# Five-stage chunk pipeline in phase A, second half of s4 issued one block later, LayerNorm statistics and evictions partly on ScalarE

## The chip, the cores and the metric

The kernel runs on one core of one Trainium2 chip. The metric is device time in microseconds (us) of a whole execution; lower is better. All times are medians of several executions. PE is the matmul engine, DVE the vector engine, ACT the scalar engine, POOL the general-purpose engine, SP the engine that issues most transfers.

Three terms recur. *Phase A* is the convolution. *The hand-over* is the stretch from the last phase-A matmul to the first matmul of s2. *Block distance* is the time from the first s2 matmul of one block to that of the next. s1(0) stands for the first s1 matmul of the first block, s1(1) for that of the second, s2(0) for the first s2 matmul.

## The reference

```python
x = A_q                                              # 2048 x 1024, bf16
for layer in range(2):
    x = x + layernorm(x) * conv(A_k, A_v)            # "A": the same conv result y both times
    z = layernorm(x); xb = z                         # "B": a mixer and an MLP
    h  = gelu(layernorm(z) @ w1)                     # 1024 -> 1024        (s1)
    xb = xb + shift4(h) @ w2                         # rows shifted by -1,+1,-2,+2  (s2)
    xb = xb + gelu(layernorm(xb) @ w3) @ w4          # 1024 -> 3584 (s3) -> 1024 (s4)
    x = x + xb
```

The convolution is a long one along the sequence, done in the kernel as FFT-like products of small matrices. Note that LayerNorm is applied to `z`, which is itself the output of a LayerNorm.

## The kernel before

Phase A works on eight chunks of 128 columns and writes y to a scratch tensor in DRAM. Two Python generators per chunk give slots of work. Most working tiles have one buffer, and the transposes share one PSUM buffer:

```python
wk  = es.enter_context(tc.tile_pool(name="a_wk", bufs=1))     # zs, z2, tm, ut ...
ptp = es.enter_context(tc.tile_pool(name="pa_t", bufs=1, space=PSUM))
# ... h_stream(c), x_stream(c): generators, one yield per stage, started 4 slots apart
```

After phase A, eight steps (2 layers x 4 blocks of 512 rows) go through these parts (shortened):

```python
def ln_stats4(src_fn):           # DVE bn_stats, bn_aggr; POOL add, pow; DVE nmr
def normalize(dst, src, rstd, nmr, t):   # ACT: Identity with scale and bias

def transposes(dst_tile, xn_tile):
    for t in range(TPB):                                   # 4 tiles of 128 rows
        pt = ps_t.tile([P, KC, P], BF16, tag="pt")         # PSUM, two buffers
        for k in range(KC):
            nc.tensor.transpose(pt[:, k, :], xn_tile[:, t, k * P:(k + 1) * P], ident[:])
        nc.vector.tensor_copy(dst_tile[:, :, t * P:(t + 1) * P], pt[:])

def pre_dve(layer, b):           # loads x and y, then
    # stats(x) -> xn0 -> x += xn0*y -> stats(x) -> xB = norm(x) -> stats(xB) -> xn
def pre_pe(layer, b):  # transposes of xn, the operand of s1
def s2_mm(layer, b):   # 64 matmuls; DVE adds; stats(xB) -> xn1 (ACT); x += xB (DVE)
def s2_pe(layer, b):   # transposes of xn1, the operand of s3
def s4(layer, b):      # two halves of 512 columns, 112 matmuls each; four DVE adds after each

for i in range(n):
    s2_mm(*steps[i])
    if i + 2 < n:
        pre_pe(*steps[i + 2]); s1(*steps[i + 2])
    s2_pe(*steps[i])
    s3(*steps[i])
    if i + 3 < n:
        pre_dve(*steps[i + 3])
    s4(*steps[i])
```

The order of the source is a priority, not the final order: the compiler's scheduler orders the instructions on each engine. The traces show the final order.

Of the kernel before, what the change touches and what calls it, by code (L numbers as in the profile page):

```python
# [87 lines left out]
def _phase_a(tc, k_in, v_in, shift_k, ssm_k, ssm_D, y_dram, ident):  # L88
# [6 lines left out]
    with ExitStack() as es:  # L95
        cp = es.enter_context(tc.tile_pool(name="a_const", bufs=1))
        inp = es.enter_context(tc.tile_pool(name="a_in", bufs=2))
        wk = es.enter_context(tc.tile_pool(name="a_wk", bufs=1))
        wk2 = es.enter_context(tc.tile_pool(name="a_wk2", bufs=2))
        bfp = es.enter_context(tc.tile_pool(name="a_bf", bufs=3))  # L100
# [31 lines left out]
        def stage1(x_c, zs):  # L132
            for a4 in range(NA // 4):
                ps = pmm2.tile([P, 4, 2, DC], F32, tag="mm2")
                for ai in range(4):
                    a = a4 * 4 + ai
                    for r in range(2):
                        nc.tensor.matmul(ps[:, ai, r, :], fwd[:, a, r, :], x_c[:, a, :], start=True, stop=True)  # L138
                asl = slice(a4 * 4, (a4 + 1) * 4)
                if RELAYOUT == "xbar":  # L140
                    evac(zs[:, :, asl, :].rearrange("p q a m -> p a q m"),
                         ps[:].rearrange("p a r (g q) -> p a q (r g)", g=G4))
                else:
                    evac(zs[:, :, asl, :].rearrange("p m a q -> p a m q"),
                         ps[:].rearrange("p a r (g q) -> p a (r g) q", g=G4))

        def relayout(zs, z2, eng):
            if RELAYOUT == "xbar":
                nc.sync.dma_start_transpose(out=z2[:], in_=zs[:].rearrange("p q a m -> p (q a m)"))
                return  # L150
            zr = zs[:].rearrange("p m a q -> p (m a q)")
            for q8 in range(NQ // 8):
                pt = ptp.tile([P, 8, P], BF16, tag="pt")
                for qi in range(8):
                    nc.tensor.transpose(pt[:, qi, :], zr[:, _sl(q8 * 8 + qi, P, NQ)], ident[:])
                evac(z2[:, q8 * 8:(q8 + 1) * 8, :], pt[:], eng)

        def zs_tile(tag):
            if RELAYOUT == "xbar":
                zt = wk.tile([P, NQ, NA, 2 * G4], BF16, tag=tag, name=tag)  # L160
            else:
                zt = wk.tile([P, 2 * G4, NA, NQ], BF16, tag=tag, name=tag)
            return zt

        def h_stream(c):
            cols = slice(c * DC, (c + 1) * DC)
            hk_c = inp.tile([P, S], BF16, tag="hk_c")
            nc.gpsimd.dma_start(hk_c[:], hv_[:, c, :])
            h_c = wk.tile([P, NA, DC], BF16, tag="h_c")
            for a8 in range(NA // 8):  # L170
                pt = ptp.tile([P, 8, P], BF16, tag="pt")
                for ai in range(8):
                    nc.tensor.transpose(pt[:, ai, :], hk_c[:, _sl(a8 * 8 + ai, P, NA)], ident[:])
                nc.vector.tensor_copy(h_c[:, a8 * 8:(a8 + 1) * 8, :], pt[:])
            nc.vector.tensor_tensor(h_c[0:1, 0, :], h_c[0:1, 0, :], dt_[0:1, cols], op=ALU.add)
            yield
            zs = zs_tile("zs_h")
            stage1(h_c, zs)
            yield
            z2 = wk.tile([P, NQ, P], BF16, tag="z2_h")  # L180
            relayout(zs, z2, "act")
            yield
            yield
            bf = bfp.tile([P, NQ, P], BF16, tag="bf")
            for blk in range(NBLK):
                bs = slice(blk * 4, (blk + 1) * 4)
                ps = pmm_d.tile([P, 4, P], F32, tag="mm")
                nc.tensor.matmul(ps[:], W_B, z2[:, bs, :], start=True, stop=True)
                evac(bf[:, bs, :], ps[:], "dve")
            bf_tiles[c] = bf  # L190
            yield

        bf_tiles = {}

        def x_stream(c):
            cols = slice(c * DC, (c + 1) * DC)
            k_nat = inp.tile([P, NT, DC], BF16, tag="k_nat")
            nc.gpsimd.dma_start(k_nat[:], kv_[:, :, cols])
            v_c = inp.tile([P, NA, DC], BF16, tag="v_c")
            nc.gpsimd.dma_start(v_c[:], vv_[:, :, cols])  # L200
# [7 lines left out]
            yield  # L208
            x_c = wk.tile([P, NA, DC], BF16, tag="x_c")
# [8 lines left out]
            yield  # L218
            zs = zs_tile("zs_x")
            stage1(x_c, zs)  # L220
            yield
            z2 = wk.tile([P, NQ, P], BF16, tag="z2_x")
            relayout(zs, z2, "dve")
            yield
            yield
            bf = bf_tiles.pop(c)
            tm1 = wk.tile([P, NQ, P], BF16, tag="tm1")
            tm2 = wk.tile([P, NQ, P], BF16, tag="tm2")
# [8 lines left out]
            yield  # L237
# [9 lines left out]
            yield  # L247
            y_c = wk2.tile([P, NA, DC], BF16, tag="y_c")
            for a8 in range(NA // 8):
# [5 lines left out]
                evac(y_c[:, a8 * 8:(a8 + 1) * 8, :], ps[:].rearrange("p a g q -> p a (g q)"), "act")  # L255
            nc.gpsimd.dma_start(yv_[:, :, cols], y_c[:])
            yield

        hs = {c: h_stream(c) for c in range(NCH)}
        xs = {c: x_stream(c) for c in range(NCH)}  # L260
        starts = []
        for c in range(NCH):
            starts.append((4 * c - 6, 1, c, hs[c]))
            starts.append((4 * c, 0, c, xs[c]))
        t_first = min(st[0] for st in starts)
        active = []
        slot = t_first
        pending = sorted(starts, key=lambda st: (st[0], st[1], st[2]))
        while pending or active:
            while pending and pending[0][0] <= slot:  # L270
                active.append(pending.pop(0))
            for item in list(active):
                try:
                    next(item[3])
                except StopIteration:
                    active.remove(item)
            slot += 1


def _b_layers(ctx, tc, x_src, y_dram, w1, w2, w3, w4, out, consts, n_layers=2):  # L280
# [16 lines left out]
    x_all = big.tile([P, NT, D], BF16, name="x_all")  # L297
# [9 lines left out]
    xv = x_src.rearrange("(t p) d -> p t d", p=P)  # L307
# [3 lines left out]
    def ln_stats4(src_fn):  # L311
        st = small.tile([P, TPB, 2, 6], F32, tag="st")
        mv = small.tile([P, TPB, 2], F32, tag="mv")
        for t in range(TPB):
# [5 lines left out]
        nc.gpsimd.tensor_scalar(ve[:], mv[:, :, 1], EPS, None, op0=ALU.add)  # L320
        rstd = small.tile([P, TPB], F32, tag="rstd")
        nc.gpsimd.tensor_tensor(rstd[:], ve[:], mhalf[:], op=ALU.pow)  # L322
        nmr = small.tile([P, TPB], F32, tag="nmr")
        nc.vector.scalar_tensor_tensor(nmr[:], mv[:, :, 0], -1.0, rstd[:], op0=ALU.mult, op1=ALU.mult)  # L324
        return rstd, nmr

    def normalize(dst, src, rstd, nmr, t):
        nc.scalar.activation(dst, src, ACT.Identity, bias=nmr[:, t:t + 1], scale=rstd[:, t:t + 1])  # L328

    def transposes(dst_tile, xn_tile):  # L330
        for t in range(TPB):
            pt = ps_t.tile([P, KC, P], BF16, tag="pt")
            for k in range(KC):
                nc.tensor.transpose(pt[:, k, :], xn_tile[:, t, k * P:(k + 1) * P], ident[:])  # L334
            nc.vector.tensor_copy(dst_tile[:, :, t * P:(t + 1) * P], pt[:])  # L335
# [3 lines left out]
    def pre_dve(layer, b):  # L339
        first = layer == 0  # L340
        T0 = b * TPB
        yt = xio.tile([P, TPB, D], BF16, tag="yt")
        for t in range(TPB):
            if first:
                nc.sync.dma_start(x_all[:, T0 + t, :], xv[:, T0 + t, :])
            nc.sync.dma_start(yt[:, t, :], yv[:, T0 + t, :])
        rstd, nmr = ln_stats4(lambda t: x_all[:, T0 + t, :])
        xn0 = xio.tile([P, TPB, D], BF16, tag="xn0")
        for t in range(TPB):
            normalize(xn0[:, t, :], x_all[:, T0 + t, :], rstd, nmr, t)  # L350
            nc.vector.tensor_tensor(xn0[:, t, :], xn0[:, t, :], yt[:, t, :], op=ALU.mult)  # L351
            nc.vector.tensor_tensor(x_all[:, T0 + t, :], x_all[:, T0 + t, :], xn0[:, t, :], op=ALU.add)  # L352
        rstd, nmr = ln_stats4(lambda t: x_all[:, T0 + t, :])
        for t in range(TPB):
            normalize(xB_all[:, T0 + t, :], x_all[:, T0 + t, :], rstd, nmr, t)
        rstd, nmr = ln_stats4(lambda t: xB_all[:, T0 + t, :])
        xn = xnp.tile([P, TPB, D], BF16, tag="xn")
        for t in range(TPB):
            normalize(xn[:, t, :], xB_all[:, T0 + t, :], rstd, nmr, t)
        state[("xn", layer, b)] = xn  # L360

    def pre_pe(layer, b):
        xnT = xtp.tile([P, KC, TB], BF16, tag="xT")
        transposes(xnT, state.pop(("xn", layer, b)))
# [54 lines left out]
    def s4(layer, b):  # L419
        h2T = state.pop(("h2T", layer, b))  # L420
        last = layer == n_layers - 1
        for half in range(2):
# [13 lines left out]
        if last:  # L436
            for t in range(TPB):
                T = b * TPB + t
                nc.sync.dma_start(ov[:, T, :], x_all[:, T, :])
# [10 lines left out]
    for i in range(n):  # L450
        s2_mm(*steps[i])
        if i + 2 < n:
# [6 lines left out]
        s4(*steps[i])  # L459
# [3 lines left out]
def kernel(  # L463
# [35 lines left out]
    _b_layers(ctx, tc, q2, y_dram[:], B_w1, B_w2, B_w3, B_w4, out2, consts)  # L499
# [30 lines left out]
```

## Time and profile before

The time before was 1462.93 us (median of 5).

| stretch | from | to | us |
|---|---|---|---|
| phase A | 0 | 283.5 | 283.5 |
| hand-over | 283.5 | 370.8 | 87.3 |
| eight blocks | 370.8 | 1461.9 | 1091.1 |

From the page of the kernel before: busy time of the engines, and the span in 40 slices, with tenths of busy time for PE and tenths of full clock for PEclk.

```profile
PE 1284.9 (88%) x7763; PEld 677.2 (46%) x7872; DVE 540.8 (37%) x1043; ACT 457.6 (31%) x562; POOL 72.9 (5%) x100
PE   3698998626899989998999899989989998998998
PEclk9799999958999999999999999999999998999999
```

The hand-over lies in the eighth to tenth slice. In the ninth PE is busy for between two and three tenths of the time, at a mean clock of 0.5. After it every third or fourth slice dips.

POOL timeline before (start, duration, what was issued; in brackets the wait before it). Chunks leave phase A 29 us apart (the last two gaps are shorter), the first at 98.6 us:

```profile
98.61 1.17 POOL L256 DMA_DIRECT2D y_scratch<-y_c  x1
127.69 1.13 POOL L256 DMA_DIRECT2D y_scratch<-y_c  x1
285.01 1.12 POOL L256 DMA_DIRECT2D y_scratch<-y_c  x1 [16.05 <-ACT y_c L128]
```

PE timeline before, in a middle block, where s2 (L397) ends and the transposes of xn (L334) begin:

```profile
796.03 10.52 PE L397 MATMUL ps<-wt,hT 128*128 128x512 bf16 x48 [0.26 <-DMA wt<-in_B_w_dram]
806.61 0.78 PE L334 MATMUL pt<-ident,xn 128*128 128x128 bf16 x11
810.15 0.61 PE L334 MATMUL pt<-ident,xn 128*128 128x128 bf16 x8 [2.76 <-DVE xnT L335]
811.83 1.71 PE L334 MATMUL pt<-ident,xn 128*128 128x128 bf16 x16 [1.07 <-DVE xnT L335]
```

The transposes wait for DVE to empty PSUM, and DVE is still busy with the adds and statistics of s2 before it comes to a copy (DVE timeline before, the same moments, two lines of many):

```profile
808.14 0.69 DVE L317 BATCH_NORM_STATS2 st<-xB_all 128x6 f32<-128x512 bf16 x1
809.46 0.64 DVE L335 COPY xnT<-pt 128x1024 bf16<-128x1024 bf16 x1
```

The three largest waits of PE before, from 365 us to the end, that is, over the eight blocks (us in total, how often, the longest):

```profile
PE pt L334 <- DVE xnT L335: 20.8, 12, 2.8
PE pt L334 <- ACT xn L328: 12.0, 3, 5.1
PE ps L375 <- DVE xn1T L335: 8.0, 8, 1.2
```

DVE and SP timelines before, at the hand-over: first statistics, normalisers ready, yt issued, first product with y.

```profile
286.24 0.69 DVE L316 BATCH_NORM_STATS2 st<-x_all 128x6 f32<-128x512 bf16 x1 [2.48 <-DMA x_all<-in_A_q_dram]
293.23 1.75 SPq L346 DMA_DIRECT2D yt<-y_scratch  x4
294.42 0.16 DVE L324 SCALAR_TENSOR_TENSOR nmr<-mv,rstd 128x4 f32<-128x4 f32 x1 [1.48 <-POOL rstd L322]
295.95 0.69 DVE L351 TENSOR_TENSOR xn<-xn,yt 128x1024 bf16<-128x1024 bf16 x1 [1.37 <-ACT xn L328]
```

Measured from the last phase-A matmul at 283.5, statistics begin after 2.7 us and the product with y after 12.4 us.

### The profile page before, as it was taken

How to read it: one execution, taken by the hardware profiler on the slowest of the kernel's cores; microseconds unless marked ns; L12 is line 12 of the kernel's file. 1: busy time of each engine (PE TensorE's matmuls, PEld its weight loads, DVE VectorE, ACT ScalarE, POOL GpSimd, SP SyncE). 2: the span in 40 equal slices, each digit the busy share in tenths (PEclk: the TensorE clock that was granted, in tenths of full speed). 3: DMA queues.
4: the chain of work that ended last, by engine and by line, in shares of the span. 5: the costliest groups of instructions: out<-in, count | busy, mean ns of one | idle time of the engine just before them, and what ended most of it. 6: DMA issues, size and time to landing. Idle time of an engine off the chain costs nothing.

```text
span 1461.9 us, 18065 instructions
## 1 busy us (share of the span) xinstructions
PE 1284.9 (88%) x7763; PEld 677.2 (46%) x7872; DVE 540.8 (37%) x1043; ACT 457.6 (31%) x562; POOL 72.9 (5%) x100
## 2 busy tenths in 40 slices
PE   3698998626899989998999899989989998998998
PEld 2577776413444444444444444444444443443443
DVE  2487878578740082028103800460040005004001
ACT  2455564346552035104510540063013201300310
POOL 1011110011100000001000100010000000000000
PEclk9799999958999999999999999999999998999999
DMA  9222320233345534544353445434443543455333
GB/s 278 59 59 60 86 60 16 75 128 114 117 149 168 156 109 140 172 144 143 117 173 116 144 144 162 137 105 144 159 158 115 158 154 120 144 163 163 108 114 115
DMA packets 166434, 188.03 MB, mean 129 GB/s; under 512 B 6225, under 2 KB 153809, under 8 KB 166098
## 3 DMA queue, kind: packets, MB, share of 16 engines
q1 hardware_dynamic: 161602, 169.05, 36.5%
q0 software_dynamic: 4608, 16.78, 4.1%
q8 instruction: 61, 1.00, 0.3%
q10 hardware_dynamic: 144, 1.05, 0.2%
q14 instruction: 19, 0.16, 0.0%
HBM read 178.46 MB, written 8.39 MB: 128 GB/s over the span
## 4 chain that ended last, share of the span: by engine, by line
issue 66%; PE 7%; POOL 3%; DVE 2%; ACT 2%; DMA 0%; POOLq 0%; SPq 0%; DVEq 0%; ACTq 0%
PE ps L375 4%; PE s L430 3%; POOL rstd L322 2%; ACT xn L328 1%; DVE st L316 1%; DVE st L317 1%; POOL ve L320 1%; DMA x_all<-in_A_q_dram 0%; ACT xB_all L328 0%; PE pt L334 0%; DVE xn L351 0%; DVE x_all L352 0%; DVE x_all L434 0%; DVE xnT L335 0%; DVE mv L318 0%
## 5 line engine op out<-in xcount | busy, mean ns | idle before, releaser
L375 PE MATMUL ps<-xn1T,wt 128*128 128x512 bf16 x1752 | 396.7, 386 | 14.8 <-DVE xn1T L335 8.0
L430 PE MATMUL s<-wt,h2T 128*128 128x512 bf16 x1760 | 387.9, 379 | 2.1
L375 PEld LDWEIGHTS <-wt 128*128 128x128 bf16 x2304 | 230.1, 100 | 305.1 <-issue 50.4
L434 DVE TENSOR_TENSOR x_all<-x_all,s 128x512 bf16<-128x512 bf16 x64 | 39.7, 682 | 722.6 <-PE s L430 722.6
L430 PEld LDWEIGHTS <-h2T 128*128 128x128 bf16 x1792 | 175.0, 98 | 211.9 <-issue 1.2
L328 ACT ACTIVATE xn<-xB_all,nmr,rstd 128x1024 bf16<-128x1024 bf16 x64 | 75.2, 1229 | 494.6 <-DVE nmr L324 490.5
L377 ACT ACTIVATE h2T<-ps 128x512 bf16<-128x512 f32 x224 | 133.4, 595 | 231.4 <-PE ps L375 217.6
L375 PE MATMUL ps<-xnT,wt 128*128 128x512 bf16 x499 | 122.5, 404 | 6.8 <-ACT hT L377 3.9
L334 PE MATMUL pt<-ident,xn 128*128 128x128 bf16 x512 | 48.6, 252 | 84.4 <-ACT xn L328 57.1
L397 PE MATMUL ps<-wt,hT 128*128 128x512 bf16 x497 | 113.0, 379 | 4.8 <-DMA wt<-in_B_w_dram 3.4
L334 PEld LDWEIGHTS <-xn 128*128 128x128 bf16 x512 | 38.8, 113 | 97.8 <-ACT xn L328 64.1
L397 PEld LDWEIGHTS <-hT 128*128 128x128 bf16 x512 | 49.9, 98 | 65.2 <-issue 7.6
L320 POOL TENSOR_SCALAR ve<-mv 128x4 f32<-128x4 f32 x32 | 7.3, 228 | 1023.6 <-DVE mv L318 1011.5
L377 ACT ACTIVATE hT<-ps 128x512 bf16<-128x512 f32 x64 | 37.8, 591 | 33.6 <-PE ps L375 33.5
L316 DVE BATCH_NORM_STATS2 st<-xB_all 128x6 f32<-128x512 bf16 x64 | 43.8, 684 | 11.6 <-ACT xB_all L328 11.1
L328 ACT ACTIVATE xB_all<-x_all,nmr,rstd 128x1024 bf16<-128x1024 bf16 x32 | 38.1, 1230 | 27.2 <-DVE nmr L324 27.2
L138 PEld LDWEIGHTS <-fwd 128*128 128x128 bf16 x512 | 35.7, 101 | 23.5 <-issue 17.8
L128 ACT ACTIVATE ut<-ps 128x1024 bf16<-128x1024 f32 x32 | 32.7, 1021 | 44.2 <-PE ps L244 44.2
L128 ACT ACTIVATE zs_x<-ps 128x1024 bf16<-128x1024 f32 x32 | 30.9, 1023 | 49.0 <-PE ps L138 49.0
L399 DVE TENSOR_TENSOR xB_all<-xB_all,ps 128x512 bf16<-128x512 bf16 x64 | 43.2, 675 | 7.1 <-PE ps L397 7.1
L328 ACT ACTIVATE xn<-x_all,nmr,rstd 128x1024 bf16<-128x1024 bf16 x32 | 38.9, 1233 | 21.1 <-DVE nmr L324 21.1
L316 DVE BATCH_NORM_STATS2 st<-x_all 128x6 f32<-128x512 bf16 x64 | 43.0, 672 | 4.0 <-DMA x_all<-in_A_q_dram 3.8
(62 smaller groups left out, 1084.5 us busy)
## 6 DMA issues: line engine op xcount, KB each, us to landing
wt<-in_B_w_dram SPq DMA_DIRECT2D x72, 1024.0 KB, 5.3
wt<-in_B_w_dram SPq DMA_DIRECT2D x144, 512.0 KB, 3.6
yt<-y_scratch SPq DMA_DIRECT2D x32, 256.0 KB, 3.8
hk_c<-in_A_ssm_k_dram POOLq DMA_DIRECT2D x8, 512.0 KB, 4.2
k_nat<-in_A_k_dram POOLq DMA_DIRECT2D x8, 512.0 KB, 5.9
v_c<-in_A_v_dram POOLq DMA_DIRECT2D x8, 512.0 KB, 5.5
y_scratch<-y_c POOLq DMA_DIRECT2D x8, 512.0 KB, 4.4
x_all<-in_A_q_dram SPq DMA_DIRECT2D x16, 256.0 KB, 5.7
```

Source lines behind the costliest of these rows:

```text
L128: nc.scalar.activation(dst, src, ACT.Copy)
L138: nc.tensor.matmul(ps[:, ai, r, :], fwd[:, a, r, :], x_c[:, a, :], start=True, stop=True)
L316: nc.vector.bn_stats(st[:, t, 0, :], src[:, 0:512])
L322: nc.gpsimd.tensor_tensor(rstd[:], ve[:], mhalf[:], op=ALU.pow)
L328: nc.scalar.activation(dst, src, ACT.Identity, bias=nmr[:, t:t + 1], scale=rstd[:, t:t + 1])
L334: nc.tensor.transpose(pt[:, k, :], xn_tile[:, t, k * P:(k + 1) * P], ident[:])
L375: nc.tensor.matmul(ps[:], wt[:, k, mi * P:(mi + 1) * P], xT[:, k, :], start=(k == 0), stop=(k == KC - 1))
L377: nc.scalar.activation(dst_fn(m), ps[:], ACT.Gelu_apprx_tanh)
L397: nc.tensor.matmul(ps[:], hT[:, k, c0:c0 + P], wts[half * 2 + k // 4][:, k % 4, :], start=(k == 0), stop=(k == KC - 1))
L399: nc.vector.tensor_tensor(xB_all[:, T, half * 512:(half + 1) * 512], xB_all[:, T, half * 512:(half + 1) * 512], ps[:], op=ALU.add)
L430: nc.tensor.matmul(pss[t][:], h2T[:, f, t * P:(t + 1) * P], wt[:, fi, :], start=(f == 0), stop=(f == FC - 1))
L434: nc.vector.tensor_tensor(x_all[:, T, half * 512:(half + 1) * 512], x_all[:, T, half * 512:(half + 1) * 512], pss[t][:], op=ALU.add)
```

## The change

It has three intents: keep more chunks of phase A in flight; shorten the hand-over; and cover the gap after s2 with matmuls of the previous block. Cut to its core:

```diff
 # phase A
-bfp = tile_pool("a_bf", bufs=3)
+wkx = tile_pool("a_wkx", bufs=2)      # zs, z2, x_c, tm1, tm2 now have two buffers
+bfp = tile_pool("a_bf", bufs=2)
-# h_stream / x_stream, one yield per stage
+# g1..g5, one yield per PSUM tile; round r runs g5(r-4), g4(r-3), g3(r-2), g2(r-1), g1(r) in turn
 # loading x
-    nc.sync.dma_start(x_all[:, T0 + t, :], xv[:, T0 + t, :])       # 16 x 256 KB, in pre_dve
+    for i in range(4):                                             # 4 x 1 MB, after phase A
+        nc.scalar.dma_start(x_all[:, i*4:(i+1)*4, :], qv[:, i*4:(i+1)*4, :])
 # transposes: eviction
-    nc.vector.tensor_copy(...)
+    if t % 2 == 0: nc.vector.tensor_copy(...)
+    else:          nc.scalar.activation(..., ACT.Copy)
 # pre_dve
+    # block 0 only: tile by tile, its stages staggered ("fine"), transposes included
-    normalize(xB_all[...], x_all[...], rstd, nmr, t)
-    rstd, nmr = ln_stats4(xB_all)                                  # third statistics, DVE
+    normalize(xB_all[...], x_all[...], rstd, nmr, t, accum=sum3[:, t:t+1])
+    nc.scalar.activation(xn[:, t, :], xB_all[...], ACT.Square, accum_out=sq3[:, t:t+1])
+    rstd, nmr = act_stats_finish(sum3, sq3)                        # six POOL operations
 # main loop
     s2_mm(*steps[i])
+    if i > 0: s4(*steps[i - 1], halves=(1,))
     ... pre_pe, s1, s2_pe, s3, pre_dve as before ...
-    s4(*steps[i])
+    s4(*steps[i], halves=(0,))
+s4(*steps[n - 1], halves=(1,))        # after the loop
```

## The prediction

> **What bounds the kernel now.** By the timeline, three stretches.
>
> *Phase A, 0 to 284 us.* y_scratch writes leave every 29.0 us per chunk; the first at 98.6. From the cadences, a chunk needs about 24 us of PE (320 matmuls of 128 columns at 0.056 to 0.064 us, 24 of 512 at 0.214), 22 of DVE (36 evictions at 0.60), 17 of ACT (18 at 0.93). No engine is full: 5 us per chunk is slot structure with single buffers. Start and drain cost more: PE does little before 23 us, and the clock is 0.61 at 40-60 us.
>
> *Hand-over, 284 to 371 us* (last phase-A matmul to first L397 matmul). PE work there is about 33 us; the table by stretches shows 2 us of PE in each of 280-300 and 300-320. The chain is stats, POOL rstd (1.04), ACT normalise (1.23 each), three times for four tiles; yt is issued only 9.6 us after the last matmul, behind the last y write.
>
> *Eight MLP blocks.* First L397 matmuls are 140.0 us apart; the matmuls need about 130 (0.219 us per 512 columns). The Trainium skill (TensorE: Matmul & The Clock Gate, Part 1) gives 0.2157 warm and a half clock after idling; the trace agrees (0.219; clock 0.74 in 1220-1240). The 10 us gap lies just after s2: transposes wait for DVE, busy with s2's adds and stats (xnT up to 2.8 us), and in the last two blocks for ACT xn (5.1 each), then run at half clock (32 transposes in 4.4 us instead of 2.2).
>
> **What the change does.**
> 1. Phase A: five groups of different chunks issued round-robin, most buffers doubled, same instructions. Steady chunk 29 to about 25.5 us, PE-bound; filling and draining stay latency-bound (pt has one buffer, about 1.8 us per use, 12 uses per chunk). The larger pools probably stop w1/w2 loading at the start, relieving the first inputs (skt took 15 us). Last matmul at about 252 instead of 283: -32.
> 2. Hand-over: block 0 per tile; third stats move from DVE (25 to 19 us per block) to ACT (12 to 16 passes of 1.23) and POOL. Yet yt still waits for the last y write, and x_all becomes 4 MB at once. Block 0 gains perhaps 3 us; blocks 1 and 2, begun meanwhile, about 10. ACT becomes the limit. -13.
> 3. s4's second half (112 matmuls, 24 us) moves after the next s2, covering s2's DVE/ACT chain of about 12 us and keeping the clock up. New: its first w4 tile waits for a wdn buffer of w2 (about 1 us), and half the transposes get ACT's slower eviction (1.02 against 0.69). Net -5 per block in the middle, -7 in the last two: -42 in all.
>
> Sum: 1463 - 32 - 13 - 42 = **1376 us**, range 1340 to 1412. Chances: faster 0.93, within 2% 0.06, slower 0.01.
>
> **What would show it.** y writes 25 to 26 us apart, last phase-A matmul near 250; first L397-type matmul 73 to 78 us after that; s2 starts 134 to 136 us apart with clock near 1.00; waits of PE for DVE xnT nearly gone; ACT busy up by about 40 us, DVE down by about 45; mean clock 0.97.
>
> **What would make it wrong.** The compiler's scheduler already reorders instructions, so phase A may keep its 29 us if pt or PSUM buffers are the true limit; or it may drain far better. The 4 MB x_all load may delay the y write and yt by several us. ACT, with gelu plus 16 long passes, could hold PSUM and stall s3. If the accumulating activations cost more than 1.23 us, or an activation table is reloaded per switch, there is no gain at the hand-over.

## The result

The changed kernel takes 1436.62 us (median of 9), against 1462.8 us of the kernel before on the same chip: ratio 0.9822, 95% interval 0.9806 to 0.9838. The prediction was 1376 us, and the measured time lies outside its range.

| stretch | before | predicted | after |
|---|---|---|---|
| phase A | 283.5 | about -32 | 254.7 (-28.8) |
| hand-over | 87.3 | about -13 | 96.8 (+9.5) |
| eight blocks | 1091.1 | about -42 | 1084.0 (-7.1) |

From the page after:

```profile
PE 1266.1 (88%) x7761; PEld 668.6 (47%) x7872; DVE 476.5 (33%) x913; ACT 522.6 (36%) x690; POOL 87.7 (6%) x162
PE   2799998057799989998999899989999999999998
PEclk9999999577899999999999999999999999999999
```

The dip of the hand-over is still there, and in one slice PE is busy for less than a tenth of the time. POOL timeline after: chunks leave 25.8 us apart while the pipeline is full, the first one 17.8 us later than before and the last one 29 us earlier.

```profile
116.40 1.12 POOL L275 DMA_DIRECT2D y_scratch<-y_c  x1 [1.43 <-ACT y_c L129]
142.20 1.12 POOL L275 DMA_DIRECT2D y_scratch<-y_c  x1 [1.09 <-ACT y_c L129]
256.14 1.12 POOL L275 DMA_DIRECT2D y_scratch<-y_c  x1 [9.62 <-ACT y_c L129]
```

PE timeline after, in a middle block (L495 is s4, L366 the transposes, L440 s1 and s3):

```profile
767.96 24.33 PE L495 MATMUL s<-wt,h2T 128*128 128x512 bf16 x109 [0.59 <-DMA wt<-in_B_w_dram]
794.82 0.27 PE L366 MATMUL pt<-ident,xn 128*128 128x128 bf16 x2 [0.64 <-DVE xnT L368]
813.10 0.61 PE L366 MATMUL pt<-ident,xn 128*128 128x128 bf16 x8 [1.72 <-DVE xn1T L368]
816.72 0.58 PE L440 MATMUL ps<-xn1T,wt 128*128 128x512 bf16 x1 [1.22 <-ACT xn1T L370]
```

s4 does fill the place after s2. But there are waits again, now at the transposes of xn1 and at the start of s3. The three largest waits of PE after, and that for xnT, same stretch and columns as before:

```profile
PE pt L366 <- DVE xn1T L368: 11.2, 10, 1.7
PE ps L440 <- ACT xn1T L370: 11.1, 8, 2.5
PE s L495 <- DMA wt<-in_B_w_dram: 9.2, 7, 2.1
PE pt L366 <- DVE xnT L368: 4.1, 6, 0.9
```

The waits named in the prediction (xnT 20.8, xn 12.0 us) have shrunk. But others stand in their place: these four lines sum to 36 us, the three of before to 41, and all waits of PE in this stretch, most of them not shown here, come to 59 us before and after. Block distances in the middle are 140.2, 142.5, 140.6 and 143.5 us, where 140.0 was before and 134 to 136 was predicted.

At the hand-over (DVE and SP timelines after; L454 is the load of w2):

```profile
251.00 2.04 SPq L454 DMA_DIRECT2D wt<-in_B_w_dram  x4
264.49 0.69 DVE L331 BATCH_NORM_STATS2 st<-x_all 128x6 f32<-128x512 bf16 x1 [9.61 <-DMA x_all<-in_A_q_dram]
265.55 1.77 SPq L378 DMA_DIRECT2D yt<-y_scratch  x4
271.37 0.69 DVE L399 TENSOR_TENSOR xn<-xn,yt 128x1024 bf16<-128x1024 bf16 x1 [2.53 <-DMA yt<-y_scratch]
```

From the last phase-A matmul at 254.7, statistics begin after 9.8 us (2.7 before) and the product with y after 16.7 us (12.4 before).

### The profile page after: what moved, and what is told of

Read it like the earlier page. It is cut to its first block, busy times and chain, and to the rows that moved or that the text cites. A ratio compares the mean times of both kernels' runs of the same rounds, so it can differ in the third digit from the quotient of the medians.

```text
span 1435.4 us, 18057 instructions
## 1 busy us (share of the span) xinstructions
PE 1266.1 (88%) x7761; PEld 668.6 (47%) x7872; DVE 476.5 (33%) x913; ACT 522.6 (36%) x690; POOL 87.7 (6%) x162
## 4 chain that ended last, share of the span: by engine, by line
PE 56%; ACT 8%; DVE 8%; DMA 5%; POOL 2%; issue 1%; another core or an unknown queue 1%; DVEq 0%; SPq 0%; ACTq 0%
PE ps L440 27%; PE s L495 25%; PE ps L462 4%; DMA wt<-in_B_w_dram 4%; ACT xn L344 2%; DVE st L332 2%; ACT xB_all L344 2%; DVE st L331 1%; ACT xn L406 1%; POOL rstd L337 1%; ACT xn1T L370 1%; DVE x_all L499 1%; DVE xn L399 1%; DVE x_all L400 1%
## 5 line engine op out<-in xcount | busy, mean ns | idle before, releaser
L440 PE MATMUL ps<-xn1T,wt 128*128 128x512 bf16 x1752 | 396.1, 385 | 19.4 <-ACT xn1T L370 11.1
L495 PE MATMUL s<-wt,h2T 128*128 128x512 bf16 x1755 | 389.1, 381 | 11.3 <-DMA wt<-in_B_w_dram 9.2
L440 PEld LDWEIGHTS <-wt 128*128 128x128 bf16 x2304 | 229.1, 99 | 312.8 <-issue 55.3
L495 PEld LDWEIGHTS <-h2T 128*128 128x128 bf16 x1792 | 175.3, 98 | 222.3 <-issue 13.0
L440 PE MATMUL ps<-xnT,wt 128*128 128x512 bf16 x437 | 103.6, 393 | 9.2 <-ACT hT L442 4.6
L366 PE MATMUL pt<-ident,xn 128*128 128x128 bf16 x512 | 44.2, 237 | 75.7 <-ACT xn L344 52.6
L366 PEld LDWEIGHTS <-xn 128*128 128x128 bf16 x512 | 36.1, 106 | 87.2 <-ACT xn L344 55.6
L335 POOL TENSOR_SCALAR ve<-mv 128x4 f32<-128x4 f32 (+1 forms) x30 | 7.1, 238 | 893.9 <-DVE mv L333 893.7
L370 ACT ACTIVATE xnT<-pt 128x1024 bf16<-128x1024 bf16 x14 | 14.3, 1019 | 95.3 <-PE pt L366 95.3
L464 DVE TENSOR_TENSOR xB_all<-xB_all,ps 128x512 bf16<-128x512 bf16 x64 | 43.2, 675 | 12.5 <-PE ps L462 12.5
L129 ACT ACTIVATE z_h<-pt 128x1024 bf16<-128x1024 bf16 x32 | 32.9, 1029 | 35.0 <-PE pt L158 34.4
L344 ACT ACTIVATE xn<-x_all,nmr,rstd 128x1024 bf16<-128x1024 bf16 x32 | 38.5, 1232 | 18.3 <-DVE nmr L339 18.3
L248 DVE TENSOR_TENSOR tm<-p,bf 128x512 bf16<-128x512 f32 x64 | 43.7, 683 | 3.9 <-PE p L245 1.9
```

The costliest lines, as they stand in the source:

```text
L129: nc.scalar.activation(dst, src, ACT.Copy)
L248: nc.vector.tensor_tensor(tm1[:, bs, :], p1[:], bf[:, bs, :], op=ALU.mult)
L344: nc.scalar.activation(dst, src, ACT.Identity, bias=nmr[:, t:t + 1], scale=rstd[:, t:t + 1], accum_out=accum)
L440: nc.tensor.matmul(ps[:], wt[:, k, mi * P:(mi + 1) * P], xT[:, k, :], start=(k == 0), stop=(k == KC - 1))
L464: nc.vector.tensor_tensor(xB_all[:, T, half * 512:(half + 1) * 512], xB_all[:, T, half * 512:(half + 1) * 512], ps[:], op=ALU.add)
L495: nc.tensor.matmul(pss[t][:], h2T[:, f, t * P:(t + 1) * P], wt[:, fi, :], start=(f == 0), stop=(f == FC - 1))
```

## The experiments

Sixteen kernels ran, each correct. The table gives medians (four executions each, three rounds against the kernel before, whose median was 1462.2 to 1464.5 us), and the three stretches read from each profiled run. A profiled run can differ from the median by some 0.4%, so stretches are compared by several us, not by one.

| run | what it is | us | ratio | phase A | hand-over | blocks |
|---|---|---|---|---|---|---|
| before | | 1462.8 | 1 | 283.5 | 87.3 | 1091.1 |
| after | the change | 1436.6 | 0.982 | 254.7 | 96.8 | 1084.0 |
| a_only | before + phase A | 1432.3 | 0.979 | 254.6 | 87.4 | 1088.0 |
| dve_stats | after, third statistics on DVE | 1429.7 | 0.978 | 253.9 | 98.7 | 1080.5 |
| dve_evict | after, evictions on DVE | 1428.6 | 0.976 | 254.8 | 92.3 | 1075.8 |
| dve_both | after, both on DVE | 1430.8 | 0.979 | 254.0 | 96.1 | 1076.6 |
| s4_old | after, s4 in its old place | 1459.6 | 0.998 | 254.6 | 96.6 | 1107.1 |
| x_pieces | after, x loaded as before | 1432.7 | 0.980 | 254.8 | 92.9 | 1086.0 |
| coarse0 | after, block 0 as a group | 1440.9 | 0.986 | 254.9 | 101.2 | 1082.3 |
| bulk_x | a_only, x in 1 MB pieces | 1437.6 | 0.983 | 254.9 | 92.5 | 1087.2 |
| act_stats | a_only, third statistics on ACT | 1435.9 | 0.982 | 254.7 | 91.4 | 1087.1 |
| a_s4 | a_only + moved half of s4 | 1421.9 | 0.973 | 254.5 | 87.5 | 1077.9 |
| order2 | a_s4, transposes inside s4 | 1382.8 | 0.945 | 254.3 | 87.1 | 1039.7 |
| wdn6 | a_s4, six weight buffers | 1407.6 | 0.962 | 254.2 | 87.0 | 1063.3 |
| no_stats3 | a_s4, no third statistics | 1401.2 | 0.958 | 254.0 | 76.2 | 1071.2 |
| comb | order2 + wdn6 | 1376.9 | 0.941 | 253.9 | 87.2 | 1032.7 |
| after_mid | after, transposes inside s4 | 1393.5 | 0.953 | 254.7 | 96.1 | 1040.4 |
| best | comb, no third statistics | 1354.1 | 0.927 | 253.8 | 76.4 | 1021.3 |

### First: which part of the change does what

**a_only**: the new phase A in the kernel before, nothing else.

```diff
-def _phase_a(...):   # of the kernel before
+def _phase_a(...):   # of the changed kernel
```

> The kernel before with only the new phase A. If phase A is worth what the trace of the change shows, its last matmul comes near 255 us instead of 284. Theory 1 (the larger phase-A pools take the room in which w2 was loaded early, so that w1, w2, x_all and yt now load together at the hand-over): the stretch from the last phase-A matmul to the first s2 matmul grows from 87 to 91-96 us and the total is 1438-1443 us. Rival (the longer hand-over of the change, 97 us, comes from its new LayerNorm code alone): the stretch stays at 87 us and the total is 1434 us.

The rival was right that the stretch would stay at 87 us: the hand-over took 87.4 us, total 1432.3. (That the LayerNorm code alone lengthens it in the change is not shown by this, see the third part.) So phase A alone gives all that the whole change gives, and everything else in the change sums to nothing or a small loss. Larger phase-A pools did not lengthen the hand-over.

**dve_stats**: third statistics back on DVE.

```diff
-normalize(..., accum=sum3[:, t:t+1]); nc.scalar.activation(..., ACT.Square, accum_out=sq3[:, t:t+1])
-st_[gi] = act_stats_finish(sum3, sq3, grp)
+normalize(...)
+st_[gi] = ln_stats4(lambda t: xB_all[:, T0 + t, :], grp)
```

> The changed kernel with the third statistics back on DVE. Theory 2 (the statistics on ACT make ACT late for gelu and for transposes): s2-to-s2 distances of 140-143.5 us in the middle fall to 135-138, s1(0) to s1(1) falls from 32.5 to about 28 us, total 1405-1418 us. Rival (moving half of s4 delays the next layer's pre-stage into s1 and s3, whichever engine does the statistics): distances stay at 140 or above, total within 6 us of 1436.

Nearly the rival: 7 us less in all, which is hardly clear of the noise (the 95% intervals of the two ratios overlap, 0.9752 to 0.9812 here and 0.9806 to 0.9838 for the change); distances 140.3, 142.7, 140.5, 142.9 us as in the change. From s1(0) to s1(1) it took 35.0 us, not 28. The statistics on ACT are not what holds the blocks.

**dve_evict**: all transposes evicted by DVE.

```diff
-    if t % 2 == 0: nc.vector.tensor_copy(...)
-    else:          nc.scalar.activation(..., ACT.Copy)
+    nc.vector.tensor_copy(...)
```

> The changed kernel with all transposes evicted by DVE again. Theory 2b (the ACT evictions, queued behind long passes, hold up the start of s1 and s3): about 2 us less per block, total 1420-1428 us. Rival (DVE evictions queue just as long behind the adds and statistics): within 4 us of 1436, either sign.

8 us less, clear of the noise and at the edge of what theory 2b said. Yet the middle distances were still 139.5 to 142.1 us.

**dve_both**: both edits at once.

```diff
+normalize(...); st_[gi] = ln_stats4(...)     # as in dve_stats
+nc.vector.tensor_copy(...)                   # as in dve_evict
```

> The changed kernel with both the third statistics and all transposes on DVE (the two single reversals gave -3.5 and -8 us in the blocks). If they are separate costs they add: s2(0) to end 1070-1073 us, total 1415-1422. If they are one cost, ACT being late, seen twice: no better than the better of the two, 1423-1429.

No better than either alone. ACT is one small cost seen twice, and it is not the main one.

**s4_old**: both halves of s4 back in their old place.

```diff
     s2_mm(*steps[i])
-    if i > 0: s4(*steps[i - 1], halves=(1,))
...
-    s4(*steps[i], halves=(0,))
-s4(*steps[n - 1], halves=(1,))
+    s4(*steps[i])
```

> The changed kernel with both halves of s4 back in their old place. If moving half of s4 pays only in the last three blocks (as the traces suggest: 4.9, 2.9 and 9.8 us lost there against 7.9, 10.4 and 13.9 before), the total grows by 8 to 15 us, to about 1448. If the move pays in all blocks and other parts of the change cost it again, it grows by 35 to 45 us. If the move hurts in the middle, it grows by less than 5 or falls.

23 us more, between the two expectations. Within the changed kernel the move is worth that much. But s4_old has 1107.1 us of blocks, where a_only, with the same order, has 1088.0. So the ACT work of the change makes the old order worse, and part of the 23 us is the repair of that. (act_stats below has ACT statistics and 1087.1 us of blocks. By this difference the ACT evictions, not the statistics, would be what hurts in the old order; no run of its own shows it.)

**a_s4**: the moved half alone, on top of a_only.

```diff
     s2_mm(*steps[i])
+    if i > 0: s4(*steps[i - 1], halves=(1,))
...
-    s4(*steps[i])
+    s4(*steps[i], halves=(0,))
+s4(*steps[n - 1], halves=(1,))
```

> The kernel before with the new phase A and the moved half of s4, nothing else of the change. If the parts add (phase A alone measured -30, the move measured -23 between two variants of the changed kernel), the total is 1405-1412 us, 25-30 us under the whole change, and the loss of the change lies in its other parts (LayerNorm on ACT, ACT evictions, block 0 per tile, x_all load). If the move pays only because it repairs what the ACT work broke, the total stays at 1425-1433.

Neither: 1421.9 us, 10 below a_only where 23 or more was expected from additivity. The middle distances, 138.8 to 140.2 us, are those of a_only (139.2 to 139.7). Only the last two blocks gain: 116.9 us instead of 123.9 in the one, and in the other 148.5 us with 24.3 us more of matmuls, instead of 127.6.

### Second: why the moved matmuls do not shorten the middle blocks

The trace of a_s4 suggests a reason. DVE timeline of a_s4 in a middle block (L449: eviction of s4, L350: eviction of transposes, L339: normaliser of the next pre-stage):

```profile
896.54 0.16 DVE L339 SCALAR_TENSOR_TENSOR nmr<-mv,rstd 128x4 f32<-128x4 f32 x1 [0.92 <-POOL rstd L337]
917.32 2.48 DVE L449 TENSOR_TENSOR x_all<-x_all,s 128x512 bf16<-128x512 bf16 x4 [20.61 <-PE s L445]
919.72 1.28 DVE L350 COPY xnT<-pt 128x1024 bf16<-128x1024 bf16 x2
939.74 0.16 DVE L339 SCALAR_TENSOR_TENSOR nmr<-mv,rstd 128x4 f32<-128x4 f32 x1 [1.47 <-POOL rstd L337]
939.82 1.28 DVE L350 COPY xn1T<-pt 128x1024 bf16<-128x1024 bf16 x2
```

PE timeline of a_s4, the same moments (L349: transposes):

```profile
920.46 1.20 PE L349 MATMUL pt<-ident,xn 128*128 128x128 bf16 x16 [1.91 <-DVE xnT L350]
940.56 0.92 PE L349 MATMUL pt<-ident,xn 128*128 128x128 bf16 x8 [2.47 <-DVE xn1T L350]
```

While s4 runs, DVE idles for 20.6 us. Both xn and xn1 are ready in that time. Yet their transposes stand after s4, and there DVE first evicts s4's four results (2.48 us), then the copies. The moved half has a second effect: the next layer's pre-stage needs the x that it completes, so the pre-stage starts when this half ends and fills DVE all through s1. At 938 us DVE waits 1.47 us for POOL's rstd of that pre-stage. The copies of xn1T, whose data is ready, stand behind it in DVE's queue. The Trainium skill (Perfetto Trace Analysis, Per-engine timelines) says that DVE and ACT are strictly first in, first out; these lines agree.

So theory 3: the gap was moved, not removed, because the transposes stayed behind. **order2** puts them where DVE idles:

```diff
-    s4(*steps[i - 1], halves=(1,))
-    ... s2_pe(*steps[i]) after s1 ...
+    s4(*steps[i - 1], halves=(1,), mid=...)   # xn1 of step i: one tile after f4 = 3, one after 4, two after 5
 ... s3, pre_dve(i + 3) ...
-    s4(*steps[i], halves=(0,))
-    ... pre_pe(i + 3) at the next step ...
+    s4(*steps[i], halves=(0,), mid=...)       # xn of step i+3: one tile after each of f4 = 1, 2, 3, 4
```

> Phase A plus moved half of s4 (the kernel of run a_s4), with the transposes of xn1 and xn issued in between the matmuls of s4, where DVE stands idle, instead of after it. Theory 3 (the gap of 10 us per block was not removed but moved: the transposes still stand at a place where DVE has the four s4 evictions and the next pre-stage before them): s2-to-s2 distances in the middle fall from 139-140 to 133-136 us, total 1385-1400. Rival (the blocks are held by ACT gelu and weights' loads): distances stay at 138 or more, total 1415 or more.

Theory 3 holds: 1382.8 us, 39 below a_s4 and slightly below the expected range, with distances 134.2, 133.9, 133.8, 133.7 us. PE timeline of order2 in a middle block:

```profile
891.09 0.61 PE L349 MATMUL pt<-ident,xn 128*128 128x128 bf16 x8
891.53 3.62 PE L445 MATMUL s<-wt,h2T 128*128 128x512 bf16 x15
894.99 0.61 PE L349 MATMUL pt<-ident,xn 128*128 128x128 bf16 x8
912.61 5.34 PE L390 MATMUL ps<-xnT,wt 128*128 128x512 bf16 x24 [1.66 <-ACT hT L392]
```

The transposes go in between matmuls without a wait. What is left are short waits for ACT's gelu (last line).

Shorter waits are not the whole gain. Over the four middle distances (a_s4, then order2; stretch, its length, busy us and instructions of PE, PEld, DVE, ACT, POOL, granted clock, DMA share, GB/s):

```profile
458.94:1017.55 558.61, 527.47 (x2561) 243.32 (x2560) 173.94 (x353) 157.34 (x208) 20.23 (x32) 0.98 0.44 141
460.01:995.66 535.65, 512.18 (x2511) 239.38 (x2560) 179.27 (x353) 155.55 (x208) 20.28 (x32) 1.00 0.47 148
```

Of the 23.0 us, 7.7 are idle time of PE and 15.3 are PE's busy time, while the mean granted clock rose from 0.98 to 1.00. The trace of order2 lacks some 50 records of matmuls, so this division is rough. From a_s4 to best, where none are missing, it is 18.3 and 14.0 us of 32.3. Fewer gaps and a higher clock came together; no run separates them. Nor does a run separate two reasons why the transposes wait less: DVE is idle there, and they no longer stand directly before the matmuls that read their result.

**after_mid** is the changed kernel, with all its ACT work, and only this new order.

```diff
 the edit of order2, made in the changed kernel
```

> The changed kernel with the transposes of xn1 and xn issued between the matmuls of s4, nothing else. Theory 3 for the change itself: middle distances fall from 140-143.5 to 133-137 us (a little more than order2's 133.8, since ACT has more to do and holds gelu), total 1395-1405. If the ACT work is what holds the blocks in the change, distances stay above 138 and the total above 1415.

1393.5 us, slightly better than expected: distances 133.4 to 133.9 us, 43 below the change. The ACT work does not hold the blocks once the transposes stand elsewhere.

**wdn6** tests the other new wait, that of s4's first weight tile for a buffer still held by s2's weights.

```diff
-wdn = tile_pool("wdn", bufs=4)
+wdn = tile_pool("wdn", bufs=6)      # room from letting xn0 and xn be one tile
```

> Run a_s4 with six wdn buffers instead of four (room from letting xn0 and xn share a tile). If the wait of the first w4 tile for a buffer of w2 costs its 0.6 to 2.8 us per block (8.3 us in all in the trace of a_s4), the total falls by 6-8 us to 1414-1416. If that wait hides others that then show in its place, by less than 3 us.

It gave 14 us, twice the expectation. The wait is gone from the list, but that is only 8.3 us. The sharing of one tile was in the same run, and where the other 6 us come from was not separated. (By the traces some 10 us of it lie in the last three blocks.) **comb** joins the edits of order2 and wdn6:

> order2 and wdn6 together. If the two waits are separate, the gains add: 7 us under order2. Otherwise within 3 us of order2.

6 us under order2: the gains add nearly as expected there, and less than the 14 us that wdn6 gave on a_s4.

### Third: the hand-over

**x_pieces** and **coarse0** undo one part each in the changed kernel.

```diff
 x_pieces:
-nc.scalar.dma_start(x_all[:, i*4:(i+1)*4, :], ...)       # 4 x 1 MB
+nc.sync.dma_start(x_all[:, T0 + t, :], xv[:, T0 + t, :]) # 256 KB, ahead of its yt tile
 coarse0:
-fine = (layer == 0 and b == 0)
+fine = False
```

> The changed kernel with x_all loaded as before: 256 KB per transfer, from SP, each just ahead of its yt tile. If the 1 MB transfers delay the first statistics (9.9 us after the last phase-A matmul against 2.7 before), s1(0) starts 40-43 us after phase A instead of 47, total down by 4-7 us. If yt and the per-tile order set the time, s1(0) stays at 45-47 us and the total within 3 us of 1436.

> The changed kernel with block 0 handled as a whole group of four tiles, as the other blocks. If the per-tile order is itself harmful (DVE stands in order behind tile 0's wait for yt while tiles 2 and 3 could be normalised), s1(0) starts 2-5 us earlier than 47 us after phase A. If the per-tile order helps as it was meant to, s1(0) starts at 52 us or later.

x_pieces: s1(0) started 43.2 us after phase A instead of 47.1, the hand-over 3.9 us shorter, total down by 4 (the total alone is within the noise). coarse0: s1(0) at 50.7 us, 3.5 later. So in the change as it is the per-tile order is not the culprit. It helps, by less than the 5 us or more that the expectation gave it.

With undoing, no single part brought the 87 us back. So each suspect was put alone into a_only. **bulk_x**:

```diff
-nc.sync.dma_start(x_all[:, T0 + t, :], xv[:, T0 + t, :])            # in pre_dve
+for i in range(4): nc.scalar.dma_start(x_all[:, i*4:(i+1)*4, :], ...)   # after phase A
```

> The kernel of run a_only (old hand-over, s1(0) 39.1 us after phase A, s2(0) 87.4) with x_all loaded in four 1 MB transfers from ACT. If the late first statistics come from the 1 MB pieces, the first statistics start 9-10 us after phase A and s1(0) moves to 43-47 us, s2(0) to 91-95. If yt hides it, s1(0) stays at 39-40.

The hand-over grew by 5.1 us to 92.5. The first statistics began at 263.03 us, 8.2 after phase A, a little sooner than expected, and s1(0) at 45.0 (DVE timeline of a_only, then that of bulk_x):

```profile
258.41 0.69 DVE L331 BATCH_NORM_STATS2 st<-x_all 128x6 f32<-128x512 bf16 x1 [3.58 <-DMA x_all<-in_A_q_dram]
```

```profile
263.03 0.69 DVE L334 BATCH_NORM_STATS2 st<-x_all 128x6 f32<-128x512 bf16 x1 [7.95 <-DMA x_all<-in_A_q_dram]
```

The Trainium skill (Trainium Kernel Development and Optimization, Key Constraints) says that transfers issued by SP, ACT and POOL run on the same 16 DMA engines and interleave. The run is in line with it: issuing x from ACT while SP loads w2 bought nothing, and a tile that used to wait for its own 256 KB now waits for 1 MB amid 4 MB of x and 2 MB of w2. The edit changed the size of the pieces, the issuing engine and how much of x is asked for at once; which of them counts is not shown.

**act_stats**:

```diff
-normalize(xB_all[...], ...); rstd, nmr = ln_stats4(xB_all)
+normalize(xB_all[...], ..., accum=sum3[:, t:t+1])
+nc.scalar.activation(xn[...], xB_all[...], ACT.Square, accum_out=sq3[:, t:t+1])
+rstd, nmr = act_stats_finish(sum3, sq3, [0, 1, 2, 3])
```

> The kernel of run a_only with the third statistics on ACT (identity with sum, square with sum) and POOL, all else old. If the ACT statistics lengthen the chain (14.7 us against 10.2 from nmr to nmr in the traces), s1(0) moves from 39.1 to 43-45 us and s2(0) from 87.4 to 91-97. If relieving DVE pays, s2(0) comes earlier than 87.

The hand-over grew by 4.0 us to 91.4. For block 0, from the second normaliser to the third (DVE timeline of a_only; then DVE and POOL timelines of act_stats):

```profile
278.56 0.16 DVE L339 SCALAR_TENSOR_TENSOR nmr<-mv,rstd 128x4 f32<-128x4 f32 x1 [1.47 <-POOL rstd L337]
287.26 0.16 DVE L339 SCALAR_TENSOR_TENSOR nmr<-mv,rstd 128x4 f32<-128x4 f32 x1 [0.91 <-POOL rstd L337]
```

```profile
279.25 0.16 DVE L339 SCALAR_TENSOR_TENSOR nmr<-mv,rstd 128x4 f32<-128x4 f32 x1 [0.92 <-POOL rstd L337]
290.45 1.01 POOL L337 TENSOR_TENSOR rstd<-ve,mhalf 128x4 f32<-128x4 f32 x1
291.42 0.20 POOL L358 TENSOR_TENSOR nmr<-m,rstd 128x4 f32<-128x4 f32 x1
```

8.7 us on DVE have become 12.2. DVE takes statistics of one tile while ACT normalises the next; on ACT the two are in series, and POOL's last step here stands behind the pow of another block (290.45). Together the two runs give 9.1 us, close to the 9.5 by which the change lengthened the hand-over. But that sum proves nothing, as the parts of the change do not add here:

- dve_stats puts the third statistics back on DVE in the change, and its hand-over is 98.7 us, not shorter than the 96.8 of the change.
- coarse0 shows that the per-tile order takes 4.4 us off the hand-over of the change. That gain is missing from the sum.
- dve_both differs from bulk_x by the per-tile order and by the moved half of s4, and that half alone left the hand-over at 87.5 us (a_s4). With the statistics on DVE the per-tile order thus made the hand-over longer, 96.1 us against 92.5. (1.6 of the 3.6 us already stand at the first statistics, which began 9.8 us after phase A instead of 8.2.)

So the statistics on ACT cost 4.0 us where block 0 is handled as a group, and nothing measurable where it is handled tile by tile.

**no_stats3**: no third statistics at all. The mean of a normalised row is 0 and its variance is v/(v+eps), so the second normaliser follows from the first.

```diff
-rstd, nmr = ln_stats4(lambda t: xB_all[:, T0 + t, :])
+r2 = rstd*rstd; r2 = r2*(-EPS) + (1 + EPS); rstd2 = r2 ** -0.5     # POOL
+rstd, nmr = rstd2, zero
```

> Run a_s4 without any third statistics: the second LayerNorm of an already normalised row is computed from the first one's variance (mean 0, variance v/(v+eps)) by three small POOL operations; correctness must hold. What the third statistics cost on DVE at all: at the hand-over s1(0) should start at 31-34 us instead of 39 after phase A, and s2(0) at 78-82 instead of 87; in the blocks at most 2 us each if DVE's queue delays the transposes. Total 1405-1415. If the hand-over is held by yt and the last y write alone, s1(0) stays at 38-39.

Correct, and 20.7 us less, 4 below the expected range: hand-over 76.2 us, better than expected, although s1(0) started at 36.1 us, later than expected; most of the gain comes in the second block, where s1(0) to s1(1) took 24.8 us instead of 32.5.

**best** is comb with the edit of no_stats3:

> comb without third statistics. If the gains add (no_stats3 gave -20.7 against a_s4, of it 11 at the hand-over; the part in the blocks may already be covered by the new order), 1357-1366 us, correct.

1354.1 us, ratio 0.9265 (0.9249 to 0.9281), correct, 3 us below the expected range and better than both kernels. Its page:

```profile
PE 1247.1 (92%) x7872; PEld 661.7 (49%) x7872; DVE 498.3 (37%) x940; ACT 454.2 (34%) x562; POOL 73.9 (5%) x108
PE   2899999458899999999999999999999999999998
PEclk9999999769899999999999999999999999999999
```

The dips between blocks are gone. That of the hand-over is shorter but still there.

## Why the prediction was wrong

The predicted direction was right. The size was not: 26 us came instead of 87.

- **Phase A: right, in part by luck.** 25.8 us per chunk (25 to 26 foretold), last matmul at 254.7 us (252 foretold), and a_only shows that the whole gain of the change is here. That a full pipeline is bound by PE holds: PE was busy for 75.2 of the 76 us from 118 to 194, against 70.4 before. But filling and draining did not stay as they were. The first y write came 17.8 us later (skt, said to be relieved, landed after 21.0 us instead of 15.1), and the last four gaps between writes shrank by 37.1 us together; the three before them by 9.5. Two errors nearly cancelled.
- **"s4's second half ... moves after the next s2, covering s2's DVE/ACT chain of about 12 us and keeping the clock up ... -42": wrong, and the main error.** The chain was covered. But "-5 per block in the middle" was nothing or worse: 140.0 us before, 140.2 to 143.5 after. The step that failed is the one from "this wait is covered" to "this time is gained". The transposes that had waited stayed behind the moved matmuls, where DVE had s4's evictions and, newly, the next layer's pre-stage in front of the copies. Alone the move gave 10 us, all in the last two blocks. With the transposes issued inside s4 the blocks fell by another 38 us in the traces (a_s4 to order2) and by 44 us in the changed kernel (after to after_mid). The distance of 134 to 136 us was a fair estimate of what the matmuls allow; the change did not reach it.
- **"Its first w4 tile waits ... (about 1 us)": right.** It was 9.2 us over seven blocks, 1.3 us each; in a_s4, where it was 8.3 us, wdn6 removed it.
- **"ACT's slower eviction": right in kind.** About 8 us, by dve_evict; with the statistics on DVE undoing it gains nothing (dve_both against dve_stats). ACT's busy time rose by 65 us rather than 40, as I had left the copies and the reading of the accumulators out of the sum. DVE's fell by 64 rather than 45.
- **The hand-over, "-13": wrong in sign.** "Block 0 gains perhaps 3 us": it lost 7.5 (s1(0) starts 47.1 us after phase A instead of 39.6). "Blocks 1 and 2 ... about 10": they lost 2.0 (49.7 us from s1(0) to s2(0) instead of 47.7). One cause is shown from both sides, and the prediction warned of it without putting it into the sum: loading x_all from ACT as 4 MB at once cost 5.1 us when added (bulk_x), and undoing it gave back 3.9 (x_pieces). The gain that should have followed from a relieved DVE did not exist: where block 0 is a group, ACT plus POOL take 12.2 us for what took DVE 8.7 (act_stats). How the rest of the 9.5 us divides between statistics, evictions and per-tile order stays open, as their costs depend on each other.
- **The clock.** I expected 0.97 as a mean and got 0.961; order2 has 0.979. The skill's half clock after idling (TensorE: Matmul & The Clock Gate, Part 1) shows here too: in the kernel before, after a wait of 5.12 us, the granted clock is 0.50 from 1229 to 1239 us. But the 4.4 us of 32 transposes there, which the prediction put down to that clock, are the pace of ACT: the four normalisations (L328) take 4.63 us, and the transposes of each tile start as its normalisation ends, 1.13 us apart. My 0.219 us per matmul was slightly wrong too: 49 matmuls take 10.74 us, the last of them 0.38, so the cadence is (10.74 - 0.38) / 48 = 0.216 us, as the page has it.

What stays open: where the other 6 us of wdn6 come from, whether the ACT evictions are all of the 19 us by which s4_old's blocks are worse than a_only's, how the hand-over's loss divides, and how much of the gain of order2 is due to the clock.

## What to carry to other kernels

When independent work is moved into a gap, ask what stood behind the gap and where it stands now. If the waiting instructions do not move to where their engine idles, and if what the moved work produces releases another burst of work, the gap only changes its place. Before moving work from a loaded engine to another, ask whether both stand in the same chain: on a chain of latency, count the steps in series, not the busy time. Split a load by what its first consumer needs: here a 1 MB piece issued from another engine did not arrive as early as a 256 KB one. And when parts of a change are measured alone, check by the reverse run that they add before naming them as causes.

## What the Trainium skill lacked or had wrong

- ScalarE: Activation LUTs (What ACT_TABLE_LOAD costs) gives an ACTIVATE's time well: for 1024 elements an estimate from its figures is 1.04 us with immediate scale and bias (measured for the squares: 1.05) and 1.23 us with two pointer operands (measured: 1.23). No page that I found says that an accumulator output adds a separate instruction: the trace has 64 ACTIVATION_READ_ACCUMULATOR of 0.19 us each, 12.3 us in all.
- GPSIMD Engine Reference gives no time for pow: here 1.01 to 1.04 us for 128x4 elements and 0.55 to 0.58 us for most of the 128x1 ones, on the chain of every LayerNorm.
- Trainium Kernel Development and Optimization, Key Constraints, is in line with the runs; it lacks a number for what a larger piece costs its first consumer under load: 256 KB pieces from SP let the first statistics start 3.8 us after the last phase-A matmul (a_only), 1 MB pieces from ACT after 8.2 us (bulk_x).
